# Convolution, LayerNorm and a two-layer network on one core: W1 split out of PSUM, a first chunk without transfers, and a new order

## The chip, the core and the metric

The kernel runs on one core of one Trainium2 chip. The time is that of one launch in device microseconds (us); the figure of a kernel is the median of its runs. Engines: PE is TensorE (PEld its weight loads), DVE is VectorE, ACT is ScalarE, POOL is GpSimd, SP issues transfers. Each engine works through its own queue in order, and waits on semaphores for the others.

## The reference

x is (8, 4224, 192), the generating weights (8, 4224, 8 heads, 7 taps), W1 (192, 768), W2 (768, 192); W1, W2 and the gain g come as float64.

```python
w = softmax(weight_gen, axis=-1)                       # 7 taps for each token and head
x_pad = concat([zeros(B, 6, 192), x], axis=1)
out = sum_k w[b,s,h,k] * x_pad[b, s+k, h, :]           # 24 channels a head
xn = (out - mean) / sqrt(var + 1e-6) * g_ln            # over the 192 channels
result = out + maximum(xn @ w_ch1, 0) @ w_ch2
```

## The kernel before

The 33,792 tokens lie on 128 partitions, 264 tokens on each. They are worked in parts of 4, 8 or 12 tokens a partition (PARTS), a part in chunks of 4 or 6 tokens; the softmax has its own blocks (SOFT, 4, 8, then 12 tokens). A group is 4 tokens of each partition; there are 66.

Softmax of a block: maximum on VectorE (tile mx), subtraction on GpSimd (e), exponential on ScalarE, sum on VectorE into the PSUM tile wn, the sum's reciprocal on ScalarE as exp(-ln) (tile rr, key rcp), two Newton rows and the product into wn on VectorE.

Convolution of a chunk (`conv`): VectorE multiplies the taps in pairs (1,2), (3,4), (5,6) into tiles pr and tap 0 into y. Within pairs 1 and 3 the halves are added by an accumulating transfer that GpSimd issues (`dma_add`, keys d0, d1). GpSimd then adds the remaining four pieces into y (keys a0 to a3).

Norm of a part (`norm`): sums and squares of each token on ScalarE (junk, s), the root and its Newton rows, then xh, its 16-bit high half (hl) on ScalarE and the low half (lo) on GpSimd. SP issues a transposing transfer of hl into xT (key turn). Transposes and accumulating transfers are kept apart: each waits for the last of the other kind that the plan has ahead of it.

The network: W1 and W2 are each held as a 16-bit high and a 16-bit low half. A group has three units of first-layer products (`wide_products`, L546, and `narrow_products`, two units together) into one of two tiles ph. ScalarE makes the ReLU's high half (hh, L576), VectorE its low half (hlo, L578); then 18 products a token (L615 to L617) into po, and VectorE adds the result to y (L628), which SP stores.

The weights (`weights`): `from_double` puts float64 words together into float32 by four VectorE rows on the integers (L689 to L699) and two ScalarE squares, the second of which also gives a row's sum of squares. W1's channels 0 to 127 are raw[0] (tile hh, 128 rows of 768), its channels 128 to 191 are raw[1], loaded as 2 blocks of 64 half rows. W2 comes in three thirds (raw[2]). `w_scale` turns a norm into a power of two through a product with ones on TensorE, a root on ScalarE and four small VectorE rows. W1's scaled float32 is written again by ScalarE, and GpSimd subtracts the high half from it. W1 stands in three blocks in the tiles c_w1h and c_w1l: channels 0 to 127, and two that pair 64 of those with the last 64, filled by 12 small transfers on SP (`shift`, L770).

The order of all of it is set by a planner (class Plan): each operation has an engine, an assumed cost, its reads and writes, and a due time `want` from the table WANT; `order()` places operations by simulated time, gives tiles from the pools (2 ph, 2 po, 5 pr, 9 y) and so fixes each engine's queue. SP waits with every transfer for the one eight transfers earlier.

Of the kernel before, what the change touches and what calls it, by code (L numbers as in the profile page):

```python
# [16 lines left out]
P = 128  # L17
# [5 lines left out]
EARLY = 0  # L23
CHUNK = 6
RING = 36
# [5 lines left out]
WANT = {'load': (-3.03, -19.38), 'wload': (75.89, -46.46), 'max': (34.08, -74.96), 'sub':  # L31
    (21.91, 116.2), 'exp': (-14.1, -87.13), 'sum': (39.61, 14.25), 'rcp': (47.36, -72.19),
    'inv': (5.5, -15.05), 'mul': (-41.29, 41.17), 'halo': (40.29, 5.8), 'c0': (31.82, 116.02),
    'c1': (-5.94, 64.81), 'c2': (-43.6, 83.75), 'c3': (-47.04, -21.22), 'd0': (9.3, 89.09),
    'd1': (-94.02, 26.89), 'a0': (-71.11, 94.32), 'a1': (-79.29, 54.26), 'a2': (-38.66, 25.11),
    'a3': (-85.55, -28.69), 'sums': (-195.22, -33.59), 'squares': (-140.38, 13.37), 'rstd':
    (10.58, 16.36), 'newton': (-103.15, -69.45), 'xh': (-25.48, -52.72), 'hi': (-57.47, -92.25),
    'lo': (-83.78, 4.64), 'turn': (28.46, -71.2), 'unit': (18.6, -32.95), 'relu': (-139.25,
# [3 lines left out]
    'w_load2': (-57.38, -12.17), 'w_as': (-60.92, -81.04), 'w_av': (-119.14, 5.54), 'w_an':  # L42
    (-33.01, 32.36), 'w_cs': (-238.15, 59.14), 'w_cv': (-62.73, -9.89), 'w_cn': (-11.28, 14.73),
    'w_c2s': (-60.02, 35.93), 'w_c2v': (-72.14, 39.45), 'w_c2n': (-110.82, -2.78), 'w_s1':
    (-187.12, 48.03), 'w_s2': (2.12, 17.57), 'w_h': (-21.92, -107.89), 'w_l': (-164.62, 27.59),
    'w_m': (-71.61, -95.38), 'w_h2': (13.94, -20.11), 'w_l2': (-164.98, -137.48)}
RAMP = 3.7
AHEAD = 0.0
WINDOW = 20.41
NEAR = 29.84  # L50
# [14 lines left out]
class Plan:  # L65
# [12 lines left out]
    def op(self, eng, cost, want, fn, r=(), w=(), lat=140.0, dma=0.0, kind=None):  # L78
# [5 lines left out]
        lead, more = WANT[want[0]]  # L84
        s = want[1]
        o.want = s - lead - more * max(0.0, 1 - s / RAMP)
# [21 lines left out]
    def order(self):  # L108
# [3 lines left out]
        last, clear = {"add": None, "turn": None}, {"add": 0.0, "turn": 0.0}  # L112
        for o in self.ops:
# [17 lines left out]
        def earliest(o):  # L131
            t = max(free[o.eng], o.ready)
            if o.kind in clear:
                t = max(t, clear[o.kind])
            for b in o.bufs:
# [12 lines left out]
        while len(out) < len(self.ops):  # L148
# [22 lines left out]
            if o.dma:  # L171
# [3 lines left out]
                dma_free[o.eng] = begin + o.dma * (1.0 if o.kind == "turn" else 1.2)  # L175
# [12 lines left out]
        return sorted(out, key=lambda o: (o.start, o.rank))  # L188
# [3 lines left out]
def kernel(  # L192
# [61 lines left out]


# [9 lines left out]
    def dma_ns(n):  # L265
        return n * P / 250.0
# [77 lines left out]
    def softmax(pa):  # L344
# [12 lines left out]
        def step(eng, cost, name, fn, r, w):  # L357
            op(eng, cost, (name, S0), fn, r, w)
# [16 lines left out]
        step("ACT", 2 * a_ns(m, 180), "rcp", ln, ["sm"], [rr])  # L375
# [11 lines left out]

# [3 lines left out]
    def conv(c):  # L391
# [3 lines left out]
        prs = {k: Buf("pr") for k in (1, 3, 5)}  # L395
# [18 lines left out]
        def mul(k, nk):  # L414
# [4 lines left out]
            if k:  # L419
# [5 lines left out]
        def add(k, E=Q):  # L425
            E.tensor_tensor(out=flat(0), in0=flat(0), in1=flat(k), op=ALU.add)  # L426
# [4 lines left out]
        nd = n * D  # L431
# [3 lines left out]
        if c < EARLY:  # L435

            for i, (k, h) in enumerate(((1, 0), (1, 1), (3, 0), (3, 1), (5, 0), (5, 1))):
                op("Pool", q_ns(nd), (f"a{max(0, i - 2)}", t0), lambda k=k, h=h: add(k + h), [(prs[k], h)], yw)
            return
        for i, k in enumerate((1, 3)):  # L440
            op("Pool", 610, (f"d{i}", t0), lambda k=k: dma_add(k, k + 1), [(prs[k], 1)],
               [(prs[k], 0)], dma=600.0 + 400.0 * n, kind="add")
# [121 lines left out]
    W1S = ["h0", "l0", "h1b", "l1b", "l2t", "h2t"] + [(k, i) for k in ("h1t", "l1t", "h2b", "l2b") for i in range(2)]  # L564
# [75 lines left out]
    for name, shape, dt in (("g", [P, 2], F32), ("gi", [P, 2], F32), ("s1", [P, 4], F32),  # L640
                            ("s2", [P, 4], F32), ("r1", [P, 4], F32), ("r2", [P, 4], F32),
                            ("fs", [P, 1], F32), ("w1h", [P, 3, F], F16), ("w1l", [P, 3, F], F16),
                            ("w2h", [P, NF, D], F16), ("w2l", [P, NF, D], F16)):
        W[name] = cp.tile(shape, dt, name="c_" + name)
    for name in ("g", "s1"):
# [8 lines left out]
    def load_weights():  # L654

        def dma(eng, E, want, dst, src, n, w):
# [4 lines left out]
            bass.AP(tensor=w1b.tensor, offset=P * 2 * F, ap=[[F, 2], [2 * F, 64], [1, F]]), 4 * F, raw[1])  # L661
        dma("ACT", A, "load", lambda: W["g"][:, 0:1], gcol[0:P, :], 200, "g0")
        for h, rows in (("t", top), ("b", bot)):
            dma("ACT", A, "load", lambda rows=rows: W["g"][rows, 1:2], gcol[P:D, :], 100, "g1" + h)
# [4 lines left out]
    def from_double(want, src, dst, n, sq, r, w, space="ph", rows=slice(0, P)):  # L669
# [3 lines left out]
        m, t = Buf("pr"), Buf(space)  # L673
# [7 lines left out]
        def tv(dt):  # L681
            a = at(t).rearrange("p a b -> p (a b)") if space == "ph" else at(t)
            return a[rows].bitcast(dt)[:, :n]
# [15 lines left out]
           lambda: V.scalar_tensor_tensor(out=dst(), in0=mv(), scalar=TINY * TINY, in1=tv(F32),  # L699
                                          op0=ALU.is_ge, op1=ALU.mult), [m, t], w)  # L700
        op("ACT", a_ns(n, 186), normed,
           lambda: A.activation(mv(), dst(), AF.Square, accum_out=sq), w, [m, (w[0], "sq")])

    def w_scale(want, ss, bound, rt, r, w):
# [4 lines left out]
        op("PE", 240, want, lambda: T_.matmul(at(pb)[:, 0:1], ones, ss, start=True, stop=True), r, [pb],  # L709
           lat=600)  # L710
# [17 lines left out]
    def weights():  # L728
        F2 = F // 2
        wac, w2r = Buf("hlo"), Buf("hlo")  # L730
        wa, wc = (wac, "a"), (wac, "c")
# [3 lines left out]
        def f32(b, n, o=0):  # L735
            if b is not w2r:
                b, o = b[0], o + (F if b[1] == "c" else 0)
            return at(b).bitcast(F32).rearrange("p j q -> p (j q)")[:, o : o + n]

        from_double("a", lambda: words(0, 0, 2 * F), lambda: f32(wa, F), F, s1[:, 0:1], [raw[0]], [wa])  # L740
        from_double("c", lambda: words(1, 0, F), lambda: f32(wc, F2), F2, s1[:, 1:2], [raw[1]], [wc])
        want = ("w_s1", 0)

        def gsum():

            for i in range(2):
                V.scalar_tensor_tensor(out=s1[:, 2 + i : 3 + i], in0=s1[:, i : i + 1], scalar=g[:, i : i + 1],
                                       in1=g[:, i : i + 1], op0=ALU.mult, op1=ALU.mult)
            V.tensor_tensor(out=s1[:, 2:3], in0=s1[:, 2:3], in1=s1[:, 3:4], op=ALU.add)

        op("V", 580, want, gsum, [(wa, "sq"), (wc, "sq"), "g0", "g1t", "g1b"], ["s1"])
        w_scale("s1", s1[:, 2:3], 128.0, r1, ["s1"], "r1")
        op("V", 130, want,
           lambda: V.tensor_scalar(out=gi, in0=g, scalar1=r1[:, 2:3], scalar2=None, op0=ALU.mult),
# [3 lines left out]
        def spare(o):  # L758
# [113 lines left out]
```

## Time and profile before

| | us |
|---|---|
| median of 3 runs | 903.32 |
| the runs | 902.16, 903.46, 903.32 |
| the profiled execution | 901.05 |
| its span in the profile | 899.2 |
| TensorE busy | 813.2 |
| VectorE busy | 781.7 |
| GpSimd busy | 694.4 |
| ScalarE busy | 675.7 |

In the profile a row names start and duration, engine, line, operation and tiles (written, then read), and in brackets the idle time just before it with what ended that. Grouped rows have count, busy time and mean duration in ns. A row of the waits says who waited for what: total us, times, longest. Lines are those of the kernel before; the numbers behind tile names in the order below are single buffers.

### The profile page before, as it was taken

Reading aid. Unit: us, or ns where it says so; the run is one execution under the profiler, and the core shown is the slowest. Engines: PE = TensorE matmul, PEld = TensorE weight load, DVE = VectorE, ACT = ScalarE, POOL = GpSimd, SP = SyncE. Lnnn points to the kernel's source line nnn. Section 1 sums busy time; section 2 is a strip of 40 time slices with the busy share of each in tenths; the row PEclk is TensorE's granted clock in tenths of the full one; section 3 lists DMA queues with packets and bytes.
Section 4 is the critical chain, followed back from the end, with each engine's and each line's share of the span. In section 5 each row is a group of like instructions: output and inputs, shape, how many; then the busy total and the mean of one; then the engine's idle time right before and its main releaser. Section 6 shows DMA issues by size and latency. Waiting matters only on the chain.

```text
span 899.2 us, 21468 instructions
## 1 busy us (share of the span) xinstructions
PE 813.2 (90%) x8716; PEld 728.8 (81%) x8716; DVE 781.7 (87%) x833; ACT 675.7 (75%) x1773; POOL 694.4 (77%) x403
## 2 busy tenths in 40 slices
PE   0037979999999999989999999999999999999997
PEld 0025969889898888888899988898899898889987
DVE  5799989999999999889999998999999799785332
ACT  1579877888878787788878778788788778788321
POOL 4499989998998896886987979689698598886000
PEclk9997999999999999999999999999999999999999
DMA  8875778878786878777788688787877867654212
GB/s 212 211 166 126 173 160 180 195 163 189 164 195 111 203 147 193 184 158 166 164 187 185 139 182 175 169 197 158 170 167 148 170 134 162 153 111 98 63 53 54
DMA packets 138604, 142.42 MB, mean 158 GB/s; under 512 B 107657, under 2 KB 109449, under 8 KB 138505
## 3 DMA queue, kind: packets, MB, share of 16 engines
q1 hardware_dynamic: 123513, 89.14, 42.0%
q0 software_dynamic: 14688, 51.91, 29.6%
q8 instruction: 68, 1.11, 0.5%
q14 instruction: 31, 0.25, 0.1%
q10 hardware_dynamic: 304, 0.00, 0.0%
HBM read 36.43 MB, written 25.95 MB: 69 GB/s over the span
## 4 chain that ended last, share of the span: by engine, by line
PE 26%; DVE 12%; POOL 9%; ACT 8%; DMA 6%; issue 5%; SPq 0%; POOLq 0%; DVEq 0%
PE ph L546 13%; POOL y L426 7%; DVE pr L423 7%; PE po L615 5%; PE po L617 4%; PE po L616 4%; DMA xT<-hl 3%; DVE hlo L578 3%; ACT hh L576 3%; ACT junk L468 2%; DMA pr<-pr 2%; ACT junk L463 1%; DVE y L423 1%; POOL hl L532 1%; DVE y L628 1%
## 5 line engine op out<-in xcount | busy, mean ns | idle before, releaser
L426 POOL TENSOR_TENSOR y<-y,pr 128x1152 f32<-128x1152 f32 (+1 forms) x204 | 503.6, 2475 | 82.0 <-DVE pr L423 70.5
L616 PE MATMUL po<-c_w2l,hh 128*128 128x192 f16 x1584 | 389.7, 246 | 1.4 <-POOL c_w2l L808 1.4
L615 PE MATMUL po<-c_w2h,hh 128*128 128x192 f16 x1584 | 390.1, 246 | 0.0
L617 PE MATMUL po<-c_w2h,hlo 128*128 128x192 f16 x1584 | 389.7, 246 | 0.0
L546 PE MATMUL ph<-xT,c_w1h 128*128 128x256 f16 x2376 | 328.3, 275 | 34.2 <-DMA xT<-hl 18.8
L423 DVE TENSOR_TENSOR pr<-x,wn 128x2304 f32<-128x2304 f32 (+1 forms) x153 | 337.4, 2215 | 8.3 <-DMA x<-in_x_dram 3.3
L546 PEld LDWEIGHTS <-c_w1h 128*128 128x128 f16 x2376 | 226.4, 98 | 76.4 <-issue 43.2
L578 DVE SCALAR_TENSOR_TENSOR hlo<-ph,hh 128x1024 f16<-128x1024 f32 x198 | 239.3, 1217 | 49.9 <-ACT hh L576 48.7
L576 ACT ACTIVATE hh<-ph 128x1024 f16<-128x1024 f32 x198 | 199.6, 1008 | 68.8 <-PE ph L546 46.0
L546 PE MATMUL ph<-xT,c_w1l 128*128 128x256 f16 (+1 forms) x1584 | 211.0, 274 | 9.8 <-DMA xT<-hl 8.9
L615 PEld LDWEIGHTS <-hh 128*128 128x128 f16 x1584 | 155.0, 98 | 7.8 <-issue 6.1
L616 PEld LDWEIGHTS <-hh 128*128 128x128 f16 x1584 | 155.1, 98 | 1.6
L617 PEld LDWEIGHTS <-hlo 128*128 128x128 f16 x1584 | 155.0, 98 | 1.6 <-issue 1.6
L514 ACT ACTIVATE xh<-y,s 128x192 f32<-128x192 f32 x264 | 123.3, 536 | 31.9 <-DVE s L502 28.3
L546 PEld LDWEIGHTS <-c_w1l 128*128 128x128 f16 (+1 forms) x1584 | 108.5, 96 | 41.8 <-issue 26.2
L532 POOL TENSOR_TENSOR hl<-xh,hl 128x768 f16<-128x768 f32 x66 | 118.8, 1868 | 15.9 <-ACT hl L530 15.8
L463 ACT ACTIVATE junk<-y 128x192 f32<-128x192 f32 x264 | 95.1, 360 | 42.4 <-POOL y L426 36.8
L468 ACT ACTIVATE junk<-y,s 128x192 f32<-128x192 f32 x264 | 119.5, 453 | 7.1
L429 POOL DMA_DIRECT2D pr<-pr x102 | 96.2, 1003 | 34.5 <-DVE pr L423 20.9
L628 DVE SCALAR_TENSOR_TENSOR y<-po,c_fs,y 128x384 f32<-128x384 f32 x132 | 79.8, 608 | 28.2 <-PE po L617 28.1
L530 ACT ACTIVATE hl<-xh 128x768 f16<-128x768 f32 x66 | 55.1, 835 | 8.2 <-DMA xT<-hl 7.6
L423 DVE TENSOR_TENSOR y<-x,wn 128x1152 f32<-128x1152 f32 (+1 forms) x51 | 60.0, 1178 | 0.0
(64 smaller groups left out, 327.2 us busy)
## 6 DMA issues: line engine op xcount, KB each, us to landing
pr<-pr POOLq DMA_DIRECT2D x60, 576.0 KB, 7.6
x<-in_x_dram SPq DMA_DIRECT2D x30, 576.0 KB, 7.0
out_dram<-y SPq DMA_DIRECT2D x30, 576.0 KB, 4.8
pr<-pr POOLq DMA_DIRECT2D x42, 384.0 KB, 6.6
out_dram<-y SPq DMA_DIRECT2D x21, 384.0 KB, 4.3
x<-in_x_dram SPq DMA_DIRECT2D x20, 384.0 KB, 6.6
w<-in_weight_gen_dram SPq DMA_DIRECT2D x21, 336.0 KB, 4.3
pr<-in_moe_w_ch_dram SPq DMA_DIRECT2D x1, 1152.0 KB
```

Source lines behind the costliest of these rows:

```text
L423: V.tensor_tensor(out=ov, in0=xv, in1=wv, op=ALU.mult)
L426: E.tensor_tensor(out=flat(0), in0=flat(0), in1=flat(k), op=ALU.add)
L463: A.activation(junk, at(y)[:, j, :], AF.Identity, scale=-1.0 / D, accum_out=at(s4)[:, 3, t : t + 1])
L468: A.activation(junk, at(y)[:, j, :], AF.Square, bias=at(s4)[:, 3, t : t + 1], accum_out=at(s4)[:, 0, t : t + 1])
L514: A.activation(at(xh)[:, t, :], at(y)[:, i, :], AF.Identity, bias=at(s4)[:, 3, g + t : g + t + 1], scale=at(s4)[:, 1, g + t : g + t + 1])
L532: lambda xh=xh, hl=hl: Q.tensor_tensor(out=halves(hl, True), in0=pairs(xh), in1=halves(hl, False), op=ALU.subtract),
L546: T_.matmul(at(gp["ph"][u])[:, r, v * 2 * P : (v + 1) * 2 * P], W[w][rows, wb, (2 * u + v) * P : (2 * u + v + 1) * P], xv[rows, r, xb, :, ...
L576: lambda: A.activation(at(hh)[:, us, :], at(ph), AF.Relu), [ph], [(hh, u)])
L578: lambda: V.scalar_tensor_tensor(out=at(hlo)[:, us, :], in0=at(ph), scalar=0.0, in1=at(hh)[:, us, :], op0=ALU.max, op1=ALU.subtract),
L615: T_.matmul(o, tok(hh, j), w2h[:, j, :], start=(j == 0), stop=False)
L616: T_.matmul(o, tok(hh, j), w2l[:, j, :], start=False, stop=False)
L617: T_.matmul(o, tok(hlo, j), w2h[:, j, :], start=False, stop=(j == NF - 1))
```

## The change

1. W1 out of float64: the words are put together in PSUM (ph for the large part, po for the small one) and stay there. The high half is scaled from PSUM as before; the low half is one VectorE row, scale times word minus high half, where ScalarE rewrote and GpSimd subtracted. Both halves share one tile w1, so 6 transfers do what 12 did. raw[1] holds each of the last 64 channels as two half rows on neighbouring partitions, in one block of 128.
2. The first chunk (EARLY is 1) has no accumulating transfers and two pairs: taps 5 and 6 are multiplied singly into ph tiles on VectorE and added to y there; GpSimd adds both pairs' halves, then the pairs, then y.
3. Scalings on ScalarE: g goes into the second square as its scale, the norm's columns are summed by TensorE, gi and the final factor fs are small ScalarE rows.
4. `hoist`: the logarithm of a sum is emitted right behind that sum, so it waits for no later VectorE row.
5. The planner: WANT has five knots over the tokens for each key, the costs of transfers and their overlap are new, SP's eight lanes are counted.

```diff
-    prs = {k: Buf("pr") for k in (1, 3, 5)}
+    prs = {k: Buf("pr") for k in ((1, 3) if c < EARLY else (1, 3, 5))}
...
+        if c < EARLY:
+            for i, k in enumerate((1, 3, 0)):
+                op("V", v_ns(2 * nd if k else nd), (f"c{i}", t0), lambda k=k: mul(k, 2 if k else 1), ...)
+            for k in (5, 6):
+                ph = Buf("ph")
+                op("V", v_ns(nd), ("c3", t0), lambda k=k, ph=ph: mul(k, 1, ph), [*xr, "wn"], [ph])
+                op("V", v_ns(nd), ("c3", t0), lambda ph=ph: V.tensor_tensor(out=flat(0), in0=bank(ph)[:, :nd], in1=flat(0), op=ALU.add),
+                   [ph], yw)
+            for i, (a, b) in enumerate((((1, 0), (1, 1)), ((3, 0), (3, 1)), ((1, 0), (3, 0)), (None, (1, 0)))):
+                op("Pool", q_ns(nd), (f"a{i}", t0), lambda a=a, b=b: add(b[0] + b[1], a[0] if a else 0), ...)
+            return
...
-            bass.AP(tensor=w1b.tensor, offset=P * 2 * F, ap=[[F, 2], [2 * F, 64], [1, F]]), 4 * F, raw[1])
+            bass.AP(tensor=w1b.tensor, offset=P * 2 * F, ap=[[F, P], [1, F]]), 4 * F, raw[1])
...
-        def low(dst, src, hi, n, r, w):
-            op("Pool", q_ns(n), ("w_l", 0), lambda: Q.tensor_tensor(out=dst(), in0=src(), in1=hi(), op=ALU.subtract), r, w)
+        def low(dst, src, scale, hi, n, r, w):
+            op("V", v_ns(n), ("w_l", 0), lambda: V.scalar_tensor_tensor(
+                out=dst(), in0=src(), scalar=scale, in1=hi(), op0=ALU.mult, op1=ALU.subtract), r, w)
...
-        copy("w_h", lambda: f32(wa, F), lambda: f32(wa, F), F, ["gi"], [wa], gi[:, 0:1])
-        copy("w_h", lambda: f32(wc, F2), lambda: f32(wc, F2), F2, ["gi"], [wc], gi[:, 1:2])
...
+        shift(w1[bot, 1], lambda: w1[top, 0], ["h0", "l0"], ["1b"])
+        shift(w1[top, 2], lambda: w1[bot, 0], ["h0", "l0"], ["2t"])
+        for i in range(2):
+            fs = slice(i * F2, (i + 1) * F2)
+            for dst, name in ((w1[top, 1, :, fs], "1t"), (w1[bot, 2, :, fs], "2b")):
+                shift(dst, lambda i=i: hlc()[i::2], [(raw[1], "h"), (raw[1], "l")], [(name, i)], F)
...
-        op("V", 580, want, gsum, [(wa, "sq"), (wc, "sq"), "g0", "g1t", "g1b"], ["s1"])
+        op("ACT", 230, want, lambda: A.activation(gi, g, AF.Copy, scale=r1[:, 2:3]), ["r1"], ["gi"])
...
-WANT = {'load': (-3.03, -19.38), ... 'turn': (28.46, -71.2), ...}
+KNOTS = (0, 4, 8, 16, 40)
+WANT = {'load': (167.46, 14.5, -216.57, -84.52, -85.06), ... 'turn': (38.15, -148.6, -103.33, 39.8, 32.55), ...}
...
-        step("ACT", 2 * a_ns(m, 180), "rcp", ln, ["sm"], [rr])
+        step("ACT", 2 * a_ns(m, 180), "rcp", ln, ["sm"], [rr], kind="next")
+    def hoist(out):
+        for o in [o for o in out if o.kind == "next"]:
+            j = out.index(o)
+            i = max(out.index(d) for d in o.deps) + 1
+            first, rest, tenants = [o], [], {(b.pool, b.slot) for b in o.bufs}
+            need, engines = set(o.deps), {o.eng}
+            for x in reversed(out[i:j]):
+                if x in need or x.eng in engines or x.dma or any((b.pool, b.slot) in tenants for b in x.bufs):
+                    first.append(x)
...
+            out[i : j + 1] = first[::-1] + rest[::-1]
```

VectorE from the first chunk's first product on, before (hh_88 and hh_89 are the two raw parts of W1):

```order
L423 TENSOR_TENSOR pr_76<-x,wn_102 128x2x768
L423 TENSOR_TENSOR pr_77<-x,wn_102 128x2x768
L361 TENSOR_REDUCE mx_93<-w_65 128x64
L423 TENSOR_TENSOR y_67<-x,wn_102 128x768
L423 TENSOR_TENSOR pr_79<-x,wn_102 128x2x768
L368 TENSOR_REDUCE wn_102<-e_97 128x64
L689 TENSOR_SCALAR ph_103<-hh_88 128x768
L361 TENSOR_REDUCE mx_92<-w_66 128x96
L692 SCALAR_TENSOR_TENSOR ph_103<-hh_88,ph_103 128x768
L689 TENSOR_SCALAR ph_104<-hh_89 128x384
L695 SCALAR_TENSOR_TENSOR ph_103<-hh_88,ph_103 128x768
L692 SCALAR_TENSOR_TENSOR ph_104<-hh_89,ph_104 128x384
```

and from the same place now:

```order
L487 TENSOR_TENSOR y_67<-x,wn_102 128x768
L487 TENSOR_TENSOR ph_103<-x,wn_102 128x768
L487 TENSOR_TENSOR ph_104<-x,wn_102 128x768
L503 TENSOR_TENSOR y_67<-ph_103,y_67 128x768
L503 TENSOR_TENSOR y_67<-ph_104,y_67 128x768
L765 TENSOR_SCALAR ph_103<-hh_88 128x768
L487 TENSOR_TENSOR pr_77<-x,wn_102 128x2x768
L768 SCALAR_TENSOR_TENSOR ph_103<-hh_88,ph_103 128x768
L771 SCALAR_TENSOR_TENSOR ph_103<-hh_88,ph_103 128x768
L775 SCALAR_TENSOR_TENSOR ph_103<-pr_78,ph_103 128x768
L423 TENSOR_REDUCE mx_93<-w_65 128x64
L487 TENSOR_TENSOR pr_79<-x,wn_102 128x2x768
```

The first chunk's last taps are single and added at once, one pair stands inside W1's rows, and the small part (hh_89) comes behind all of the large one.

GpSimd around the first group's low half, before:

```order
L426 TENSOR_TENSOR y_68<-y_68,pr_79 128x768
L767 TENSOR_TENSOR c_w1l<-hlo_90,c_w1h 128x768
L767 TENSOR_TENSOR hh_89<-hlo_90,hh_89 128x384
L426 TENSOR_TENSOR y_68<-y_68,pr_79 128x768
L532 TENSOR_TENSOR hl_83<-xh_81,hl_83 128x2x384
L426 TENSOR_TENSOR y_68<-y_68,pr_80 128x768
L426 TENSOR_TENSOR y_68<-y_68,pr_76 128x768
```

and now:

```order
L490 TENSOR_TENSOR y_68<-y_68,pr_78 128x768
L490 TENSOR_TENSOR y_68<-y_68,pr_80 128x768
L605 TENSOR_TENSOR hl_83<-xh_81,hl_83 128x2x384
L493 DMA pr_78<-pr_78 128x768
L493 DMA pr_79<-pr_79 128x768
L490 TENSOR_TENSOR y_69<-y_69,pr_80 128x768 x2
L425 TENSOR_TENSOR e_97<-w_64,mx_93 128x672
L605 TENSOR_TENSOR hl_84<-xh_82,hl_84 128x2x384
```

The second chunk's sum is complete ahead of the low half, the third chunk's two accumulating transfers stand right behind it, and the second group's low half follows five rows later.

SP's last rows of the start, now, with their waits (DMASW3 is the fourth accumulating transfer):

```order
L838 DMA c_w_121<-hh_89 64x2x384 [waits DMAHW7_49]
L838 DMA c_w_121<-hh_89 64x2x384 [waits DMAHW0_49]
L609 DMA_TRANSPOSE xT_85<-hl_83 128x12x128 [waits DMAHW1_49,DMASW3_49,Pool_49]
L609 DMA_TRANSPOSE xT_86<-hl_84 128x12x128 [waits DMAHW2_49,Pool_49]
L397 DMA x<-in_x_dram 128x1x768 [waits DMAHW3_49]
```

The first transpose waits for the later of those two transfers, and the second transpose now stands directly behind the first, where three loads of x stood between them before.

More of the change, by code (lines that the diff above doesn't have):

```diff
@@ L22 @@
 SOFT = (4, 8) + (12,) * 21
-EARLY = 0
 CHUNK = 6
+EARLY = 1
 RING = 36
@@ L187, in order @@
             out.append(o)
-        return sorted(out, key=lambda o: (o.start, o.rank))
+        out.sort(key=lambda o: (o.start, o.rank))
+        return self.hoist(out)
+    @staticmethod
+    def hoist(out):
[7 more added lines that the diff above has]
+                    first.append(x)
+                    need |= x.deps
+                    engines.add(x.eng)
+                    tenants |= {(b.pool, b.slot) for b in x.bufs}
+                else:
+                    rest.append(x)
+            out[i : j + 1] = first[::-1] + rest[::-1]
+        return out
 @with_exitstack
```

187 lines of the change are left out of this document (101 added, 86 removed), and 14 rows, old and new, of the table WANT.

## The prediction

> **What bounds the kernel now.** I read the page first, then windows of the span, then TensorE's rows and the other engines in order of time up to 110 us, then the waits.
>
> ```profile
> span 899.2 us, 21468 instructions
> PE 813.2 (90%) x8716; PEld 728.8 (81%) x8716; DVE 781.7 (87%) x833; ACT 675.7 (75%) x1773; POOL 694.4 (77%) x403
> ```
> ```profile
> 0.00:25.00 25.00, 0.00 (x0) 0.00 (x0) 11.35 (x19) 4.12 (x8) 11.94 (x14) 1.00 0.81 195
> 25.00:50.00 25.00, 0.59 (x2) 0.61 (x3) 22.38 (x42) 15.60 (x43) 12.94 (x10) 1.00 0.80 207
> 50.00:75.00 25.00, 12.82 (x82) 8.63 (x82) 24.53 (x34) 20.80 (x61) 23.19 (x17) 0.80 0.79 171
> 75.00:100.00 25.00, 21.83 (x217) 18.67 (x217) 23.66 (x33) 22.07 (x59) 25.00 (x17) 0.93 0.63 138
> 100.00:200.00 100.00, 93.83 (x1017) 84.56 (x1016) 95.88 (x108) 81.28 (x227) 94.14 (x64) 1.00 0.80 174
> 200.00:300.00 100.00, 98.58 (x1069) 88.80 (x1067) 97.38 (x102) 83.97 (x223) 89.96 (x53) 1.00 0.78 172
> ```
> ```profile
> 83.07:100.00 16.93, 16.93 (x184) 14.96 (x184) 16.60 (x25) 14.56 (x36) 16.93 (x13) 1.00 0.67 150
> ```
> ```profile
> 83.07:893.68 810.61, 794.64 (x8599) 715.87 (x8598) 715.79 (x731) 627.69 (x1639) 638.28 (x361) 1.00 0.72 156
> ```
> The columns are the stretch, its length, busy time (and count) of PE, PEld, DVE, ACT and POOL, granted clock, DMA share, GB/s. From 83.07 to its last product at 893.68 TensorE is busy 794.64 of 810.61 us: there it is the bound, with 16.0 us of holes. Up to 100 us it has done 301 of 8716 matmuls, so the start is where time can be had. But from 100 to 300 us VectorE is busy 95.9 and 97.4%: a TensorE that starts earlier soon waits for VectorE, unless VectorE is ahead too.
>
> ```profile
> 53.02 1.44 PE L546 MATMUL ph<-xT,c_w1h 128*128 128x256 f16 x6 [18.76 <-DMA xT<-hl]
> ...
> 70.01 0.61 PE L546 MATMUL ph<-xT,c_w1l 64*128 64x256 f16 x4 [6.03 <-DMA xT<-hl]
> ...
> 81.57 0.24 PE L616 MATMUL po<-c_w2l,hh 128*128 128x192 f16 x1 [1.38 <-POOL c_w2l L808]
> ```
> TensorE starts at 53.02, then stands for the second transposed group until 70.01 and for the low half of W2 until 81.57. Only then does it run through.
>
> ```profile
> 26.75 0.56 DVE L689 TENSOR_SCALAR ph<-hh 128x384 int32<-128x384 int32 x1 [7.12 <-DMA hh<-in_moe_w_ch_dram]
> ```
> ```profile
> 24.00:26.10 2.10, 0.00 (x0) 0.00 (x0) 0.00 (x0) 0.00 (x0) 1.60 (x1) 1.00 0.13 53
> ```
> At the root of it, VectorE stands 7.12 us until the small second load of W1 (384 KB) lands at 26.7. From 24.0 to 26.1 the DMA share is 0.13 of 16 engines, about two: this load, whose source pattern has 2 as its outermost size, drains through two engines alone.
>
> **The change part by part.** Durations, by groups of one line and shape:
>
> ```profile
> L426 POOL TENSOR_TENSOR y<-y,pr 128x768 f32<-128x768 f32 x18 | 35.3, 1962 | 5.4 <-DVE pr L423 3.3 <-DMA pr<-pr 1.6
> L423 DVE TENSOR_TENSOR pr<-x,wn 128x1536 f32<-128x1536 f32 x17 | 29.3, 1746 | 3.6 <-DMA x<-in_x_dram 3.3 <-ACT rr L372 0.3
> L423 DVE TENSOR_TENSOR y<-x,wn 128x768 f32<-128x768 f32 x6 | 5.6, 941 | 0.0
> L578 DVE SCALAR_TENSOR_TENSOR hlo<-ph,hh 128x1024 f16<-128x1024 f32 x4 | 4.9, 1216 | 0.9 <-POOL c_w2l L808 0.9
> L808 POOL TENSOR_TENSOR c_w2l<-hlo,c_w2h 128x1152 f16<-128x1152 f32 x1 | 3.0, 2968 | 0.0
> L767 POOL TENSOR_TENSOR c_w1l<-hlo,c_w1h 128x768 f16<-128x768 f32 x1 | 1.6, 1630 | 0.0
> L800 DVE SCALAR_TENSOR_TENSOR c_fs<-c_r,c_r 128x1 f32<-128x1 f32 x1 | 1.2, 1240 | 0.0
> L749 DVE TENSOR_TENSOR c_s<-c_s 128x1 f32<-128x1 f32 x1 | 1.2, 1217 | 0.0
> L689 DVE TENSOR_SCALAR ph<-hh 128x768 int32<-128x768 int32 x1 | 1.0, 951 | 0.0
> L764 ACT ACTIVATE hlo<-hlo,c_gi 128x768 f32<-128x768 f32 x1 | 0.9, 920 | 0.0
> ```
> VectorE's own work. Added: the first chunk's last two products go singly through PSUM, four rows of 0.94 instead of one pair at 1.75, +2.0 us. No row of before adds out of PSUM into SBUF; the nearest are L689, which writes PSUM (0.95), and L578, which reads it (1.216 for 1024, so 0.91 for 768). The low halves of W1 come over from GpSimd, 0.95 and 0.56: +1.5. Removed: the sum of squares (1.22) and the final factor (1.24), -2.5, and three rows under 0.4, left out. Net +1.0 at most, paid for by the 7.12 us.
>
> The loads. Both W1 loads now stand ahead of two loads of softmax weights, and the second has 128 outermost. With 112 + 924 KB ahead, 1152 KB of its own and 195 GB/s it lands about 11 us after the first issue, near 13, long before VectorE asks for it near 22. If it drained as before, to 26.7, VectorE would stand 4 us; I take the spread, by the 0.13, and keep 4 for the range. The Trainium skill ("DMA: Bandwidth & Descriptors", Rules for kernel authors) says that the slowest dimension of a transfer's patterns sets how many engines carry it, and an outermost size under 16 confines it to that many. The 0.13 agrees for a size of 2; by that rule the new load uses all 16 and the sum stands, without it the forecast would be 899.8.
>
> VectorE in its new order. Rows that follow closely start 0.08 us before the one ahead ends.
>
> ```profile
> 9.95 3.42 DVE L423 TENSOR_TENSOR pr<-x,wn 128x1536 f32<-128x1536 f32 x2 [3.25 <-DMA x<-in_x_dram]
> ...
> 98.22 1.74 DVE L423 TENSOR_TENSOR pr<-x,wn 128x1536 f32<-128x1536 f32 x1
> ```
> From the same 9.95, adding durations row by row: the first chunk's single products and additions to 14.4; both W1 matrices, two pairs and the second softmax to 25.3; two pairs of the second chunk to 28.7; a maximum, a product and W1's scale to 31.0; a pair 32.7; a sum, which waits for an exponential until 33.2, to 34.1; the low halves 35.5; W2's rows and the first Newton steps 41.3; then two pairs of the third chunk with a W2 row between, 45.2. Over the next 58 rows, with one stand of 1.4 for a ReLU behind ScalarE's sums, the seventh chunk's last pair, eight hlo rows and three final rows are done near 93. Before, the same set is done with the row at 98.22 and a final one, at 100.4. **VectorE is 7 us ahead.**
>
> GpSimd loses the first chunk's two transfer issues and both subtractions for W1 (1.63 and half of it) and gains nothing.
>
> ```profile
> 47.48 1.64 POOL L532 TENSOR_TENSOR hl<-xh,hl 128x768 f16<-128x768 f32 x1
> ...
> 98.67 2.19 POOL L426 TENSOR_TENSOR y<-y,pr 128x768 f32<-128x768 f32 x1
> ```
> The first chunk is summed at 28.5 (four adds of 1.8 behind a subtraction that ends at 21.4), the first group's low half is ready at 44.0 instead of 49.1, and the sixth chunk is summed near 94.3 instead of 100.9. **GpSimd is 5 to 7 us ahead.**
>
> The first transpose is where the change adds a wait. Two accumulating transfers are now issued right behind that low half, and the transpose waits for both to land; SP's later loads queue behind it. The second waits for VectorE's pair at 45.2. Landing of such transfers (first row) and of a transpose (second), up to 110 us:
>
> ```profile
> DMA to landing us min/median/max: 3.8/6.9/10.7
> ```
> ```profile
> DMA to landing us min/median/max: 3.2/3.2/3.3
> ```
> So TensorE starts at 52.2 to 59.1; little else is in flight then, I take 5.5 and 54.0, a microsecond later than now. But the second transpose follows at once (57.7 instead of 70.0), and W2's low half is done near 65 instead of 81.5: its scale leaves VectorE at 56.0, two passes on ScalarE end at 62.7, then L808. Units 1 to 4 are paced by their hlo rows, which end at 60, 63, 68 and 70, so up to 3 us of a later start are covered by VectorE. By 81.3 TensorE has done 210 matmuls of the two layers; before, 297 by 100.0 (301 less 4 of the norms), and at 0.092 each (16.93 us for 184) the 210th falls at 92. **TensorE is 10 to 11 us ahead.**
>
> Logarithms behind sums: ScalarE's own order is as planned either way; only what the logarithm waits for moves, from a later VectorE row to the sum.
>
> ```profile
> ACT rr L372 <- DVE pr L423: 3.4, 2, 2.7
> ...
> ACT rr L372 <- DVE y L423: 2.1, 3, 1.5
> ```
> These 5.5 us lie on ScalarE, idle a quarter of the span: 0 to 2 on the path, I take 0.5. Its new scalings (three small rows) against the two lost copies (0.92 and half of it) are worth under a microsecond beside other work: 0.
>
> The rest of the plan: the products of a group and the rows behind 893.68 are the same, so 0. The 16.0 us of holes are of this kind:
>
> ```profile
> PE ph L546 <- DVE hlo L578: 13.0, 15, 3.1
> PE ph L546 <- DMA xT<-hl: 2.9, 3, 1.6
> ```
> A new table may remove most of them (-12) or make half as many again and more (+10); nothing in the trace picks a side: 0.
>
> The sum: TensorE's lead lasts only as far as the supply's 5 to 7 carry it, with VectorE near full to 300 us. I take 7.0, and 0.5 from the logarithms: 899.2 - 7.5 = 891.7. The profiled execution took 901.05, 2.27 under the median of 903.32; off the median, **895.8 us**.
>
> **Rivals.** First, the new order also closes most holes. 13.0 us of them wait for hlo rows queued behind pairs on VectorE, which finer placing can mend; against it, VectorE has little slack before 300. Half to all of 16.0 more is 880 to 888, say 887. Chance 0.20.
>
> Second, the supply gives little back: VectorE has as many rows as before, and if other waits in its order eat the lead, or the W1 load still drains slowly (4 us), 0 to 3.5 remain: 900 to 903, say 901.5. Chance 0.17.
>
> Third, slower, by transposes behind adds. If what happens at the first transpose is the plan's habit, TensorE waits for landings of 6.9 again and again. Of each, about 2.5 would show behind the products still in hand, so with three the 7.5 is gone; five give 908. For it: the 2.9 us of such waits now. Against: in the new order the adds that most later transposes wait for stand two to five rows ahead of the low half. Chance 0.11.
>
> **How the numbers follow.** Forecast 895.8, chance 0.52, own range 891 to 899.5 (landing, supply of 5 to 10, holes within 3). With two in ten outside, 885.5 to 903. A measurement of this kernel tells 0.2%, 1.8 us, from no change. Faster: 0.52, 0.20 and 0.09 of the second rival, 0.81; same 0.07; slower 0.01 and the third's 0.11, 0.12.
>
> **What would show it.** Right: no 7 us stand of VectorE before 27 us, the first group's low half near 44, TensorE's first products near 54, the second transpose near 58, W2's low half near 65, no TensorE wait over 3 us after 70. Wrong: VectorE stands elsewhere before 45 us, the first transpose lands after 60, or the holes from 100 to 800 us are not 10 to 22.

## The result, and the profile after

The kernel after takes 917.63 us (median of 4 runs, 914.73 to 920.22) beside 903.39 for the kernel before on the same chip: ratio 1.0168, 95% interval 1.0149 to 1.0187. By the ratio it is 1.7% slower; the forecast was 895.8. The profiled execution has a span of 914.3 us.

The first two lines of its page, then its windows (stretch, length, busy time and count of PE, PEld, DVE, ACT and POOL, granted clock, DMA share, GB/s):

```profile
span 914.3 us, 21469 instructions
...
PE 819.2 (90%) x8722; PEld 732.7 (80%) x8722; DVE 781.6 (85%) x832; ACT 675.9 (74%) x1774; POOL 691.3 (76%) x399
```
```profile
0.00:100.00 100.00, 41.34 (x379) 34.32 (x380) 85.80 (x127) 62.76 (x175) 71.96 (x53) 1.00 0.73 172
100.00:200.00 100.00, 87.12 (x915) 76.66 (x913) 86.28 (x101) 74.02 (x205) 84.12 (x58) 0.97 0.75 162
200.00:300.00 100.00, 93.55 (x1012) 84.18 (x1010) 95.73 (x98) 81.78 (x214) 87.90 (x53) 1.00 0.78 166
300.00:800.00 500.00, 489.62 (x5251) 439.86 (x5250) 455.56 (x439) 400.04 (x1057) 412.06 (x217) 0.99 0.77 166
```

By 100 us TensorE has done 379 matmuls where it had done 301: at 0.092 us each it is 7.2 us ahead. From 100 to 200 it does 915 instead of 1017, and from 200 to 300 it does 1012 instead of 1069, so at 300 us it is 81 behind (2306 to 2387). The lead was there and was lost between 100 and 300; 57 more matmuls are lost from 300 to 800, where the kernel before did 5308. From 100 to 800 TensorE is idle for 29.7 us (12.88, 6.45 and 10.38).

The start, in rows of the engines' timelines (start, duration, engine, line, operation; in brackets the idle time ahead):

```profile
12.87 1.33 ACT L762 ACTIVATE pr<-hh 128x384 f32<-128x384 f32 x2 [7.14 <-DMA hh<-in_moe_w_ch_dram]
25.21 3.42 DVE L487 TENSOR_TENSOR pr<-x,wn 128x1536 f32<-128x1536 f32 x2
45.23 1.65 POOL L605 TENSOR_TENSOR hl<-xh,hl 128x768 f16<-128x768 f32 x1
56.02 8.72 PE L619 MATMUL ph<-xT,c_w 128*128 128x256 f16 x60 [1.55 <-DMA xT<-hl]
64.87 2.38 POOL L870 TENSOR_TENSOR c_w2l<-hlo,c_w2h 128x1152 f16<-128x1152 f32 x1 [0.97 <-ACT c_w2h L868]
```

W1's small load has landed at 12.87, VectorE takes up the second chunk at 25.21, the first group's low half ends at 46.88, TensorE begins the layers at 56.02 with 60 matmuls in one go, and W2's low half ends at 67.25. All of this is within 3 us of the forecast. One stand was not in it: ahead of 43.42 VectorE stood 2.84 us for an addition on GpSimd, which had itself stood 5.38 us for an accumulating transfer. The waits (total, times, longest; the last row is of the kernel before) show what went wrong later:

```profile
PE ph L619 <- DVE hlo L651: 34.5, 28, 6.4
DVE y L487 <- ACT rr L434: 14.0, 4, 5.0
DVE pr L487 <- issue: 8.6, 4, 5.5
PE ph L619 <- DMA xT<-hl: 1.7, 2, 1.5
```
```profile
PE ph L546 <- DVE hlo L578: 16.2, 17, 3.1
```

TensorE waits 34.5 us for hlo rows (before, 16.2). VectorE waits 14.0 us, in 4 stands, for the logarithm on ScalarE, and 8.6 us more for something that the profile does not name; without the hoist (below) 0.9 us of that is left. The worst place, on three engines:

```profile
103.82 1.00 ACT L649 ACTIVATE hh<-ph 128x1024 f16<-128x1024 f32 x1
105.38 0.32 ACT L434 ACTIVATE rr<-wn,bias 128x96 f32<-128x96 f32 x1
```
```profile
105.80 1.75 DVE L487 TENSOR_TENSOR pr<-x,wn 128x1536 f32<-128x1536 f32 x1 [5.51 <-issue]
...
110.00 2.35 DVE L651 SCALAR_TENSOR_TENSOR hlo<-ph,hh 128x1024 f16<-128x1024 f32 x2
```
```profile
111.27 6.39 PE L619 MATMUL ph<-xT,c_w 128*128 128x256 f16 x40 [6.44 <-DVE hlo L651]
```

VectorE stands 5.51 us and starts 0.10 us after the logarithm ends at 105.70. The ReLUs that the next two hlo rows need were done by 104.82, but these rows stand behind three products in VectorE's queue and run from 110.00; TensorE stands 6.44 us for it. In the built program that product has a wait for ScalarE, for the semaphore value that this logarithm sets, and without the hoist it has none. The two rows, after and then without the hoist:

```
L487 TENSOR_TENSOR pr1_77<-x_63,wn0_102 128x2x768 [waits DMASW1_49,DMAHW2_49,Activation_49,Pool_49]
L487 TENSOR_TENSOR pr1_77<-x_63,wn0_102 128x2x768 [waits DMAHW2_49,DMASW1_49,Pool_49]
```

The tile wn holds the softmax's weights, which the products read, and the sums, which the logarithm reads. The program orders rows of two engines on this tile as they are emitted, although here both only read. Emitted late, the logarithm waits for the products ahead of it; emitted early, the products behind it wait for the logarithm, wherever ScalarE's queue has it. At 105.38 it had ReLUs and eight squares and sums ahead of it.

The Trainium skill ("PSUM — Partial Sum Buffer", PSUM bank collisions raise a hardware error) says that two engines on one PSUM bank collide, reads with reads too, so that something has to keep them apart. By the code this product reads columns 224 to 447 of wn and the logarithm 672 to 767, which is not one bank by the 2 KiB (512 columns) that this page of the Trainium skill gives a bank: the wait here is wider than that rule asks. The products of a block's last tokens do reach past column 511, into the logarithm's bank. No run here shows a collision, and a narrower wait within PSUM was not tried.

### The profile page after: what moved, and what is told of

Its sections match the earlier page's. It is cut to its first block, busy times and chain, and to the rows that moved or that the text cites. A ratio compares the mean times of both kernels' runs of the same rounds, so it can differ in the third digit from the quotient of the medians.

```text
span 914.3 us, 21469 instructions
## 1 busy us (share of the span) xinstructions
PE 819.2 (90%) x8722; PEld 732.7 (80%) x8722; DVE 781.6 (85%) x832; ACT 675.9 (74%) x1774; POOL 691.3 (76%) x399
## 5 line engine op out<-in xcount | busy, mean ns | idle before, releaser
L490 POOL TENSOR_TENSOR y<-y,pr 128x1152 f32<-128x1152 f32 (+1 forms) x201 | 491.7, 2447 | 98.0 <-DVE pr L487 85.4
L619 PE MATMUL ph<-xT,c_w 128*128 128x256 f16 (+1 forms) x3960 | 438.4, 275 | 36.4 <-DVE hlo L651 34.5
L619 PEld LDWEIGHTS <-c_w 128*128 128x128 f16 (+1 forms) x3960 | 335.4, 98 | 114.0 <-issue 75.3
L487 DVE TENSOR_TENSOR pr<-x,wn 128x2304 f32<-128x2304 f32 (+1 forms) x152 | 336.0, 2218 | 14.2 <-issue 8.6
L605 POOL TENSOR_TENSOR hl<-xh,hl 128x768 f16<-128x768 f32 x66 | 113.8, 1757 | 19.5 <-ACT hl L603 19.4
L493 POOL DMA_DIRECT2D pr<-pr x100 | 93.6, 977 | 23.6 <-DVE pr L487 13.9
L536 ACT ACTIVATION_READ_ACCUMULATOR junk<-y 128x1 f32 x264 | 49.4, 187 | 0.0
L541 ACT ACTIVATION_READ_ACCUMULATOR junk<-y,s 128x1 f32 x264 | 49.4, 187 | 0.0
```

What stands on the lines that cost most here:

```text
L487: V.tensor_tensor(out=ov, in0=xv, in1=wv, op=ALU.mult)
L490: Q.tensor_tensor(out=flat(to), in0=flat(to), in1=flat(k), op=ALU.add)
L536: A.activation(junk, at(y)[:, j, :], AF.Identity, scale=-1.0 / D, accum_out=at(s4)[:, 3, t : t + 1])
L541: A.activation(junk, at(y)[:, j, :], AF.Square, bias=at(s4)[:, 3, t : t + 1], accum_out=at(s4)[:, 0, t : t + 1])
L605: lambda xh=xh, hl=hl: Q.tensor_tensor(out=halves(hl, True), in0=pairs(xh), in1=halves(hl, False), op=ALU.subtract),
L619: T_.matmul(at(gp["ph"][u])[:, r, v * 2 * P : (v + 1) * 2 * P], W[w][rows, wb, (2 * u + v) * P : (2 * u + v + 1) * P], xv[rows, r, xb, :, ...
```

## The experiments

All times, with the ratio to the kernel before, timed beside each of them (903.4, 902.4, 903.5, 903.8 and 903.1 us in five sets of runs), and its 95% interval:

| kernel | us | ratio |
|---|---|---|
| after | 917.6 | 1.0168 (1.0149 to 1.0187) |
| after, no hoist | 901.4 | 0.9984 (0.9965 to 1.0002) |
| before, with the hoist | 915.5 | 1.0144 (1.0124 to 1.0165) |
| after, sums in SBUF | 957.8 | 1.0612 (1.0582 to 1.0641) |
| before, sums in SBUF | 940.6 | 1.0420 (1.0400 to 1.0441) |
| after, three logarithms hoisted | 896.6 | 0.9931 (0.9908 to 0.9955) |
| after, logarithm moved on ScalarE too | 896.2 | 0.9906 (0.9870 to 0.9942) |
| after's code, old planner, no hoist ("old order") | 891.5 | 0.9859 (0.9829 to 0.9889) |
| after, no hoist, old load of W1 | 903.2 | 0.9983 (0.9965 to 1.0001) |
| new planner, old table, no hoist | 930.3 | 1.0299 (1.0266 to 1.0332) |
| old planner, new table, no hoist | 938.1 | 1.0374 (1.0343 to 1.0405) |
| new planner, old table from token 16, no hoist | 942.2 | 1.0428 (1.0395 to 1.0461) |
| old order, logarithm moved on ScalarE too | 898.3 | 0.9945 (0.9925 to 0.9965) |
| old order, first chunk as before | 897.6 | 0.9937 (0.9916 to 0.9958) |
| old order, old load of W1 | 898.5 | 0.9947 (0.9926 to 0.9969) |
| old order, with the hoist | 899.3 | 0.9954 (0.9936 to 0.9972) |

### After, without the hoist

```diff
-        return self.hoist(out)
+        return out
```

> The kernel after with the hoist left out: every engine's rows stand in the same order, only the places in the program at which the logarithms are emitted, and so the waits between ScalarE and VectorE on the tile wn, go back. Theory A (the hoist turns the logarithm's wait into a wait of VectorE: a product that stands behind an early logarithm may not start before ScalarE has taken it, and ScalarE has ReLUs ahead of it; VectorE stood 5.5, 3.7, 2.4, 4.9 and 5.1 us so, and the hlo rows behind it held TensorE): those stands go, TensorE's holes fall from 37.5 us to about 20, and the time to 898 to 904 us. Theory B (the new order loses the lead whatever the logarithms do: hlo rows queued behind pairs): 3 us at most come back, 913 to 918 us, and TensorE still stands over 5 us near 105.

901.38 us. The stands go, as theory A has it. In the two built programs the rows of every engine stand in the same order, and only waits differ. The same place (VectorE, ScalarE, TensorE) and two of its waits:

```profile
99.88 1.75 DVE L487 TENSOR_TENSOR pr<-x,wn 128x1536 f32<-128x1536 f32 x1
...
104.08 2.35 DVE L651 SCALAR_TENSOR_TENSOR hlo<-ph,hh 128x1024 f16<-128x1024 f32 x2
```
```profile
105.06 0.32 ACT L434 ACTIVATE rr<-wn,bias 128x96 f32<-128x96 f32 x1
```
```profile
105.82 4.32 PE L619 MATMUL ph<-xT,c_w 128*128 128x256 f16 x40 [1.32 <-DMA xT<-hl]
```
```profile
PE ph L619 <- DVE hlo L651: 19.7, 31, 3.4
ACT rr L434 <- DVE pr L487: 10.0, 5, 5.3
```

The logarithm runs at nearly the same time, 105.06, but VectorE has done the product at 101.63 and the hlo rows run 5.9 us earlier. ScalarE now waits 10.0 us for products, which costs far less than VectorE's stands did: TensorE's wait for hlo rows falls from 34.5 to 19.7. By the ratios the hoist costs 1.84%, 16.6 us.

### Before, with the hoist alone

The same function and the logarithm's mark, put into the kernel before.

> The kernel before with the hoist alone; each engine's order is that of before. Theory A: in this order ScalarE reaches most logarithms at about the time that VectorE reaches the row that now waits, since the logarithms' waits behind later rows were 5.5 us in all; so VectorE stands 0 to 3 us at a place and the time is 902 to 907 us. Theory B: the hoist is worth what the prediction gave it, 0.5 us: 902 to 904 us. A time over 907 would say that the hoist costs by itself in any order.

915.52 us, far more than either theory gave. The last sentence of the expectation holds in this order too: the hoist costs by itself.

```profile
PE ph L566 <- DVE hlo L598: 25.2, 17, 5.6
DVE pr L443 <- ACT rr L392: 9.6, 2, 5.3
DVE y L443 <- ACT rr L392: 1.7, 2, 0.9
```

My estimate of 0 to 3 us a place was taken from ScalarE's short waits at logarithms; how long ScalarE takes to come to them was not in that row.

### The sums in an SBUF tile, in both kernels

```diff
-        sm = WN[:, S0_ : S0_ + m]
+        sm = SM[:, :m]
```

> The kernel after (hoist kept) with the softmax's sums in a small SBUF tile of their own instead of the PSUM tile wn that also holds the weights; orders are the same. No product shares a tile with the logarithm any more, so neither waits for the other. Theory A: as without the hoist or a little better, 896 to 903 us, no stand of VectorE behind a logarithm. Theory B: 912 to 917 us.

> The kernel before with the sums in an SBUF tile of their own. Both theories: the waits between logarithms and products go, 2.2 us of VectorE near 128 us and some tenths elsewhere: 900 to 903.5 us. It says what the shared tile costs without the change.

957.77 and 940.63 us: both theories missed, for a reason that neither held. The rows on the sums became long (first row: after, second and third: with sums in SBUF):

```profile
L440 DVE SCALAR_TENSOR_TENSOR wn<-wn,rr 128x96 f32<-128x96 f32 (+2 forms) x23 | 5.8, 252 | 0.8 <-ACT rr L435 0.6
```
```profile
L441 DVE SCALAR_TENSOR_TENSOR sm<-sm,rr 128x96 f32<-128x96 f32 (+2 forms) x23 | 44.5, 1934 | 0.6 <-ACT rr L436 0.6
...
L442 DVE SCALAR_TENSOR_TENSOR sm<-sm,rr 128x96 f32<-128x96 f32 (+2 forms) x23 | 26.8, 1165 | 0.8
```

They hide what the shared tile costs in time. But VectorE's stands for the logarithm are gone: where the kernel after waited 14.0 and 8.6 us, its waits with the sums in SBUF name only the 0.6 us of the first Newton row for the reciprocal, which it had as well. So the stands came from the shared tile. The last section comes back to the long rows.

### Three logarithms hoisted; the logarithm moved on ScalarE too

```diff
-        for o in [o for o in out if o.kind == "next"]:
+        logs = [o for o in out if o.kind == "next"]
+        for o in (logs[7], logs[9], logs[10]):
```

> The kernel after with the hoist kept for three logarithms alone, the 8th, 10th and 11th of 23: without the hoist ScalarE waited 2.9, 5.3 and 3.6 us at these for a later VectorE row, and with it VectorE waited 0.4 to 0.5. Theory A (a wait should be left with the engine that has the slack at that place): the hole of 3.7 us that TensorE had near 279 without the hoist closes, 895 to 900 us, 2 to 5 under the kernel without the hoist. Rival C (waits of ScalarE at logarithms are covered by its idle quarter): as without the hoist, 900 to 903.

```diff
-            first, rest, tenants = [o], [], {(b.pool, b.slot) for b in o.bufs}
...
-            out[i : j + 1] = first[::-1] + rest[::-1]
+            tenants = {(b.pool, b.slot) for b in o.bufs}
+            for k in range(i, j):
+                if any((b.pool, b.slot) in tenants for b in out[k].bufs):
+                    i = k + 1
+            out.insert(i, out.pop(j))
```

> The kernel after, but the logarithm moves in ScalarE's own queue too: it stands there right behind the last row emitted ahead of the sum, in front of the ReLUs and squares that the hoist moved along with it. Theory A: VectorE's next row on wn then waits for a short ScalarE row and not for ReLUs, so stands of 5 us do not occur; VectorE loses 0.4 to 1 us at each of 15 sums, which partly shows, and ScalarE waits for sums now and then: 898 to 907 us. Theory D (any early logarithm costs, since VectorE has to wait at all): 910 or more.

896.64 us: three hoisted logarithms do not cost and gain 0.5%. That is inside theory A's range, but not by its mechanism, and where the gain comes from is not shown. The hole that theory A saw close is still there, in ScalarE's, GpSimd's and TensorE's rows of the kernel with three:

```profile
268.94 2.63 POOL L491 TENSOR_TENSOR y<-y,pr 128x1152 f32<-128x1152 f32 x1 [1.40 <-DMA pr<-pr]
```
```profile
271.60 0.36 ACT L537 ACTIVATE junk<-y 128x192 f32<-128x192 f32 x1 [3.68 <-POOL y L491]
277.88 1.00 ACT L650 ACTIVATE hh<-ph 128x1024 f16<-128x1024 f32 x1
```
```profile
281.45 2.93 PE L620 MATMUL ph<-xT,c_w 128*128 128x256 f16 x13 [4.51 <-DVE hlo L652]
```

It is not the hoist's: without any hoist TensorE stands 3.42 us ahead of 283.15. ScalarE waits 3.68 us for a chunk that GpSimd finishes late, then does its twelve sums and squares, 6.3 us, and the ReLU behind them comes at 277.88.

896.20 us with the logarithm moved in ScalarE's queue as well, a little under theory A's range: in this order early logarithms do not cost as such (theory D falls). With the hoist they cost because ReLUs and squares stood ahead of them.

```profile
ACT rr L428 <- DVE wn L424: 21.8, 19, 3.9
PE ph L613 <- DVE hlo L645: 20.9, 25, 2.2
```

Now ScalarE does the waiting, 21.8 us for the sums, and TensorE's longest wait for an hlo row is 2.2.

### The order: old and new planner on the same code

The kernel after without the hoist, with WANT, RAMP, WINDOW, NEAR and the transfers' costs and overlap of before, and without the count of lanes:

> The code of the kernel after without the hoist, ordered by the table, window and assumed transfer costs of before: the new split of W1, the first chunk and the scalings alone, in an order that was not made for them. If the lead at the start comes from these parts, TensorE's 210th matmul still starts 6 us or more earlier than before and the time is 896 to 902 us. If it comes from the new table's order (W1's loads ahead of softmax weights, W2's scale early), the 210th starts within 3 us of before and the time is 901 to 908 us.

891.53 us, the fastest of all, 1.4% under before and below both ranges. So on this code, without the hoist, the new order costs 0.9984 - 0.9859, 1.25% or 11.3 us. The windows without the hoist, in the new order and in the old one:

```profile
0.00:100.00 100.00, 40.75 (x383) 34.27 (x384) 86.06 (x128) 63.04 (x176) 72.07 (x53) 1.00 0.73 172
100.00:200.00 100.00, 94.62 (x1005) 83.84 (x1003) 94.44 (x112) 79.84 (x223) 93.32 (x64) 0.98 0.86 179
200.00:300.00 100.00, 93.12 (x984) 83.17 (x982) 94.09 (x93) 81.17 (x214) 86.80 (x50) 0.98 0.81 165
300.00:800.00 500.00, 493.34 (x5321) 443.62 (x5319) 461.83 (x447) 404.25 (x1065) 411.43 (x219) 1.00 0.78 165
```
```profile
0.00:100.00 100.00, 39.83 (x366) 33.17 (x367) 88.54 (x130) 65.84 (x185) 76.33 (x56) 0.91 0.78 185
100.00:200.00 100.00, 95.31 (x1026) 85.17 (x1025) 94.39 (x112) 82.03 (x222) 88.55 (x61) 1.00 0.76 166
200.00:300.00 100.00, 96.72 (x1031) 86.77 (x1029) 96.14 (x95) 80.47 (x217) 91.46 (x52) 0.98 0.78 174
300.00:800.00 500.00, 496.78 (x5380) 448.01 (x5378) 465.74 (x451) 410.27 (x1083) 419.14 (x223) 1.00 0.79 166
```

The new order starts better (383 matmuls to 366 by 100 us) and is 110 matmuls behind by 800 us (7693 to 7803, 10.1 us). TensorE is idle 18.9 us from 100 to 800 in the new order and 11.2 in the old; the place near 277 is one of these holes. The old order does not simply keep a lead either: against the kernel before it is 65 matmuls ahead at 100 us, 36 at 300 and 108 at 800.

Table and planner were then taken apart:

> The kernel after without the hoist, its planner with the new costs, lanes and window, but the due times of before (two numbers for each key). It splits the 9.9 us between the kernel with everything of the old planner (891.5) and the one with the new (901.4). If the new table of due times loses them: 889 to 895 us. If the new costs and window do: 898 to 904 us.

> The other half of the split: the code of after without the hoist, the new table of due times, but the costs of transfers and the window of the planner before. If the new table loses the 9.9 us: 898 to 906 us. If the new costs and window do: 889 to 895 us.

> The kernel after without the hoist, the new table for what belongs to the first 16 tokens of a partition and the due times of before from token 16 on; costs and window new. If the new table loses in the long middle (ReLUs behind squares of a chunk that GpSimd finished late, as near 277 us), the lead of 12 us at the 210th matmul holds better and the time is 888 to 896 us. If the lead is lost because VectorE is full up to 300 us, whatever the table, it is 898 to 903 us.

930.32, 938.13 and 942.22 us, all far outside what either answer gave. The 11.3 us can be put down to neither half: all three mixtures of one planner's table with the other's costs and window, or of the two tables, are 26 to 38 us slower than before. Which entries lose the lead in the new order stays open.

> The code of after in the order of the old planner (891.5 us), with the logarithms moved to right behind the last row ahead of the sum in ScalarE's own queue. In that order ScalarE idled 11.0 us and VectorE 0.4 us at logarithms, so there is little to take: 888 to 893 us. If VectorE's short waits at every sum show in full, 894 to 897 us.

898.33 us, outside the first range, a little above the second and 0.86% over the old order: moving the logarithm on ScalarE too is not free in every order. ScalarE's waits at logarithms rise from about 11 us to 18.4; how that reaches TensorE is not shown.

### What the parts bring, and the hoist in a third order

The load, in the new order without the hoist and in the old order. Both kernels leave out the places that the old load needs in the rows behind it, so only their times are of use:

```diff
-            bass.AP(tensor=w1b.tensor, offset=P * 2 * F, ap=[[F, P], [1, F]]), 4 * F, raw[1])
+            bass.AP(tensor=w1b.tensor, offset=P * 2 * F, ap=[[F, 2], [2 * F, 64], [1, F]]), 4 * F, raw[1])
```

> The kernel after without the hoist, with W1's small second load read as before, 2 blocks of 64 half rows, in place of 128 half rows in order (so the last 64 channels' rows stand on other partitions than the products take them for). The step of the prediction on loads: it lands past 20 us instead of near 13; if it drains to 26, VectorE stands some 4 us before its rows, and the time is 2 to 5 us over the kernel without the hoist, 903 to 907. Rival: in the new order nothing asks for it before it lands anyway, within 1 us of the kernel without the hoist.

> The code of after in the order of the old planner, its order unchanged, with W1's small second load read as 2 blocks of 64 half rows (the last 64 channels' rows stand on other partitions than the products take them for). In this order VectorE asks for it at 18.4 us. The prediction's step: it lands past 24, VectorE and the rows of W1 behind it stand 4 to 8 us, and the time is 895 to 900 us. Rival: a stand at the start is eaten by TensorE's later waits, 890 to 893 us.

In the new order the load makes no difference to the time (0.9983 to 0.9984), though VectorE stands 3.52 us for it (by way of a square on ScalarE), near the 4 of the prediction, and TensorE begins the layers at 58.60 instead of 56.37. In the old order it costs 0.88%, 8.0 us, and one can follow it (VectorE, GpSimd, TensorE; first with the old load, then with the new one):

```profile
25.11 0.56 DVE L728 TENSOR_SCALAR po<-hh 128x384 int32<-128x384 int32 x1 [6.03 <-DMA hh<-in_moe_w_ch_dram]
```
```profile
45.19 1.64 POOL L568 TENSOR_TENSOR hl<-xh,hl 128x768 f16<-128x768 f32 x1
```
```profile
50.29 6.23 PE L582 MATMUL ph<-xT,c_w 128*128 128x256 f16 x40 [18.88 <-DMA xT<-hl]
```
```profile
38.52 1.64 POOL L568 TENSOR_TENSOR hl<-xh,hl 128x768 f16<-128x768 f32 x1
```
```profile
43.62 5.98 PE L582 MATMUL ph<-xT,c_w 128*128 128x256 f16 x40 [18.88 <-DMA xT<-hl]
```

A stand of 6.03 us, a low half 6.67 later, a TensorE start 6.67 later, and by the ratios 8.0 at the end. That a stand was free in the new order fits a lead that was lost there anyway.

The first chunk as before (EARLY = 0):

> The code of after in the order of the old planner (891.5 us), with the first chunk done as before: three pairs, two accumulating transfers (the planner places the rest again, so its order differs from the first chunk on). If the first chunk carries the lead: the first group's low half is 3 us later or more and the time 894 to 900 us. If W1's split and load carry it: 890 to 893 us. A time over 905 would only say that the table does not suit this code.

897.61 us, inside the first range, but not by its mechanism: the low half was ready 0.6 us earlier, not later, and the planner placed everything behind it anew. What the first chunk brings is not settled by this.

> The code of after in the order of the old planner, with the hoist. Without it ScalarE idled 11.0 us and VectorE 0.4 us at logarithms. Theory A: the hoist hands waits to VectorE whatever the order, 10 us or more in all, and TensorE stands for the hlo rows behind: 899 to 908 us. If it costs only in orders that place ScalarE's logarithms badly: 890 to 894 us.

899.26 us: 0.95%, 8.6 us, in the third order too, and the waits are of the same kind:

```profile
DVE pr L450 <- ACT rr L397: 8.4, 3, 4.0
...
DVE y L450 <- ACT rr L397: 1.6, 1, 1.6
```

## Why the prediction was wrong

By the ratios, the change of +1.68% (+15.2 us; the two medians differ by 14.2) is the sum of three along one path: the code in the old order -1.41% (-12.7), the new order +1.25% (+11.3), the hoist +1.84% (+16.6). The first share also holds the old planner's new placing of the changed code. On another path the shares differ: the hoist cost 1.44% on the kernel before and 0.95% in the old order.

- **The start** was right. W1's load near 13 (12.87); VectorE's walk to 25.3 (25.21); TensorE's start at 54.0 (56.02, inside its range); W2's low half near 65 (67.25); 210 matmuls of the layers by 81.3 (210). The first group's low half was forecast ready at 44.0 and ended at 46.88. VectorE had its set of rows done at 94.5 (near 93 forecast), 6.0 us ahead of before, and GpSimd its 24th addition at 96.5, 4.3 ahead instead of 5 to 7. One of the listed signs against it came: VectorE stood 2.84 us before 45. The prediction says that no row of before adds out of PSUM into SBUF; L628 does, at 0.61 us for 384 columns. The 0.94 taken for 768 held (0.95). How much of the 7.0 in the sum was right can't be read off one run: the code was worth 12.7 us in the old order, but only part of that is a lead from the start.
- **"Logarithms behind sums", 0.5 gained,** is the step that failed, with the largest size: it cost 16.6 us (13.0 and 8.6 in the two other orders). The sentence "only what the logarithm waits for moves, from a later VectorE row to the sum" is true and is half of it. A wait between two rows that the program orders does not go: taken off ScalarE, idle a quarter of the span, it came to VectorE, which had been 95.9% busy from 100 to 200 us. The prediction priced who stopped waiting and did not ask who waits instead, or what is queued behind that row: hlo rows.
- **"The rest of the plan", 0,** is the second: 11.3 us, just outside its bounds (-12 to +10). The choice of 0 was wrong, and what in the new order costs it stays open. As the prediction's last part had it, holes outside 10 to 22 us would speak against it: they are 29.7 between 100 and 800 us, 18.9 without the hoist.
- **The rivals.** The third had the sign and not the cause: TensorE waits for transposed groups 1.7 us in all, so no transposes behind adds. The second, that other waits in the order eat the lead, is near what is left without the hoist: 901.4, for its 900 to 903. A slower kernel through VectorE behind ScalarE was not among them.

## What to carry to other kernels

A row that is emitted earlier so as to wait less makes others wait for it, if both touch one tile: look at what then stands behind it on the engine that is nearly full, and move the row in its own engine's queue as well or not at all; in the old order even that cost 0.86%. A new order has to be timed against the old one on the same code before a part of the change is credited or blamed; here the code was worth 12.7 us in the old order and the order that came with it took back 11.3. A lead at the start decides little by itself: kernels with 366, 383 and 387 matmuls at 100 us (old order, no hoist, first chunk as before) took 891.5, 901.4 and 897.6 us. Due times moved from one planner to the other made all three mixtures 26 to 38 us slower.

## What the runs showed of the hardware

Small VectorE rows with both operands in SBUF waited for GpSimd. In the kernel after with the sums in SBUF the first Newton row took 1.93 us in the mean where it took 0.25 with one operand in PSUM. Thirteen of the 46 rows of the two Newton steps had no GpSimd row beside them and took 0.19 to 0.26 us; most of the long ones ended 0.08 to 0.14 us after a GpSimd row. One took 7.35 us, and ended 0.14 us after the third of three GpSimd rows that followed each other:

```profile
391.88 7.35 DVE L441 SCALAR_TENSOR_TENSOR sm<-sm,rr 128x96 f32<-128x96 f32 x1
```
```profile
392.01 2.93 POOL L491 TENSOR_TENSOR y<-y,pr 128x1152 f32<-128x1152 f32 x1
394.60 1.93 POOL L606 TENSOR_TENSOR hl<-xh,hl 128x768 f16<-128x768 f32 x1
396.20 2.89 POOL L491 TENSOR_TENSOR y<-y,pr 128x1152 f32<-128x1152 f32 x1
```

The Trainium skill ("SBUF — State Buffer", SBUF: two separate sides) says that a VectorE row with two SBUF inputs and a GpSimd row that reads SBUF share one pair of ports, that the one that starts first has it for its whole instruction, and that the other waits. The waits agree; here one VectorE row was not let in between three GpSimd rows either, though by the profile it started 0.13 us ahead of the first of them.

Most long stands of TensorE cost more than their length. The 40 matmuls behind the one of 6.44 us took 6.39 us, and 40 of the same kind took 4.32 without the hoist, behind a stand of 1.32. The windows of the two stretches show the granted clock at 0.65 and at 1.00:

```profile
111.27:117.66 6.39, 6.39 (x43) 4.40 (x42) 6.29 (x11) 4.47 (x13) 4.07 (x4) 0.65 0.36 86
```
```profile
105.82:110.14 4.32, 4.32 (x42) 3.54 (x43) 4.22 (x10) 3.83 (x13) 4.11 (x5) 1.00 0.83 187
```

The other two stands over 3 us of the kernel after, 3.13 us ahead of 501.33 and 3.73 ahead of 728.64, have a granted clock of 0.51 and 0.74 in the 3 us behind them; the one of 3.15 us in the kernel before, ahead of 133.57, has 1.00.
